# Holding back a batch's loads, with v in runs of four tokens, k chunks of every second row, and v's tail compact

## The chip, the cores and the metric

The kernel runs on one core of one Trainium2 chip. The metric is the device time of one execution in microseconds (us). A run is called slow when its time is over 1.5% above the fastest run of the same kernel in its job, and fast otherwise; the mean clock that the chip granted to the tensor engine is given beside it. Where not said otherwise, only fast runs are compared. Engine names follow the profile: PE is the tensor engine, PEld its weight loads, DVE the vector engine, ACT the scalar engine, POOL the general engine, SP the engine that here does nothing but start DMAs. "SPq" lines are DMAs that SP issued; their time is what the issue took on SP's own queue, not the time to landing.

## The reference

An attention layer with a learned feature map, then a gated linear unit with a causal convolution of five taps. Shapes: 8 batches, 8 heads, 576 tokens, head size 64, 128 features, model size 512, all float32.

```python
def _attn_ref(q, k, v, w_phi):
    def phi(x):
        proj = np.einsum('bhsd,df->bhsf', x, w_phi)
        proj = proj - np.max(np.abs(proj), axis=-1, keepdims=True)
        return np.concatenate([np.exp(proj), np.exp(-proj)], axis=-1)
    q_p, k_p = (phi(q), phi(k))
    kv = np.einsum('bhsf,bhsd->bhfd', k_p, v)
    z = np.sum(k_p, axis=2)
    num = np.einsum('bhsf,bhfd->bhsd', q_p, kv)
    den = np.einsum('bhsf,bhf->bhs', q_p, z)[..., None] + 1e-06
    return (num / den).astype(np.float32)

def _moe_ref(x, w_val, conv_w, w_out):
    # gate = sigmoid(causal convolution of x with conv_w, 5 taps, per channel)
    # val = x @ w_val
    return (gate * val @ w_out).astype(np.float32)
```

## The kernel before

The main loop is a pipeline of three stages over batches. Iteration i makes the features of k and q of batch i, the attention of batch i-1 and the gated unit (called MLP below) of batch i-2. The instructions of the stages are interleaved in the program, so PE's queue holds them in one fixed order.

First, k and q are cast to bfloat16 by POOL into a scratch buffer in DRAM, and SP reads them back with a transposing DMA. A batch's loads and transposes are put into the program at the start of the iteration before.

```python
def load_rows(st, src, name, parts):
    b = st.b
    T = qtp.tile([P, H * HALF], BF16, name=name)
    rows = src[b].rearrange("h s d -> h (s d)").rearrange("h (i x) -> i h x", x=256)
    hn = H // parts
    for c in range(parts):
        R = dram.tile([hn * 2 * P, 2 * D], BF16, name=f"{name}R{parts}")
        nc.gpsimd.dma_start(
            R[:, :].rearrange("(h i y) x -> i h (y x)", h=hn, y=2), rows[0:P, c * hn:(c + 1) * hn, :],
        )
        nc.sync.dma_start_transpose(T[:, c * hn * 2 * P:(c + 1) * hn * 2 * P], R[:, :])
    # ... the same for the tail (the last 64 tokens of each head), name "...Rt"
```

Second, v comes by plain DMAs on SP: two for the main part, and eight small ones for the tail, into a tile with zeros between the heads, so that one matmul can serve four heads.

```python
    for hq in range(4):
        for g in range(2):
            nc.sync.dma_start(
                st.VNt[32 * hq:32 * hq + 32, 2 * g:2 * g + 2, hq, :],
                v[b, 4 * g + hq, 4 * P:S, :].rearrange("(r t) d -> r t d", t=2),
            )
```

Third, the features come in five units, u = 4 (the tail) first. POOL multiplies v by the exponentials of each unit (tile VT; VTt for the tail), and PE accumulates k features times v in `unit_kv`.

Fourth, the results leave by `unit_out`, three times per batch. ACT copies a PSUM tile into an SBUF tile OUTs, and SP stores it. The pool that OUTs comes from has two buffers. All PSUM tiles share one pool of four.

```python
    mlp = ctx.enter_context(tc.tile_pool(name="mlp", bufs=2))
    ps2 = ctx.enter_context(tc.tile_pool(name="ps2", bufs=4, space=bass.MemoryType.PSUM))
    # ...
def unit_out(st, w):
    # ... matmuls into OUTp ...
    OUTs = mlp.tile([P, 2, DM], FP32, name="OUTs")
    nc.scalar.activation(OUTs[0:m, 0:len(cs), :], OUTp[0:m, 0:len(cs), :], AF.Copy)
    for n, c in enumerate(cs):
        # ... (two, three and one store for w = 0, 1 and 2)
            nc.sync.dma_start(ob[par, i0:i0 + k, :], OUTs[n0 - P * c:n0 - P * c + k, n, :])

for i in range(B + 2):
    # sa, sb, sc: states of batches i, i-1, i-2
    if i + 1 < B:
        load_qk(states[i + 1])
        load_v(states[i + 1])
    if sa:
        alloc_A(sa)
        alloc_B(sa)
    merge(units_features(sa) if sa else [], units_mlp(sc) if sc else [])
    if i == 0:
        late_constants()
    num = units_num(sb) if sb else []
    if sa:
        unit_mrows(sa)
        kv = units_kv(sa)
        merge(units_q(sa), num[0:3] + kv[0:1] + num[3:6] + kv[1:2] + num[6:])
```

Of the kernel before, what the change touches and what calls it, by code (L numbers as in the profile page):

```python
# [19 lines left out]
P = 128  # L20
# [13 lines left out]
def kernel(  # L34
# [13 lines left out]

    nc = tc.nc
# [19 lines left out]
    def load_rows(st, src, name, parts):  # L69
        b = st.b  # L70
        T = qtp.tile([P, H * HALF], BF16, name=name)
        rows = src[b].rearrange("h s d -> h (s d)").rearrange("h (i x) -> i h x", x=256)
        hn = H // parts
        for c in range(parts):
            R = dram.tile([hn * 2 * P, 2 * D], BF16, name=f"{name}R{parts}")
            nc.gpsimd.dma_start(
                R[:, :].rearrange("(h i y) x -> i h (y x)", h=hn, y=2), rows[0:P, c * hn:(c + 1) * hn, :],
            )
            nc.sync.dma_start_transpose(T[:, c * hn * 2 * P:(c + 1) * hn * 2 * P], R[:, :])  # L79
        R = dram.tile([H * NT, 2 * D], BF16, name=f"{name}Rt")  # L80
        nc.gpsimd.dma_start(
            R[:, :].rearrange("(h i y) x -> i h (y x)", h=H, y=2), rows[P:HALF // 2, :, :],
        )
        nc.sync.dma_start_transpose(T[:, TAIL:H * HALF], R[:, :])
        return T

    VNT = []
    for s in range(2):
        t = const.tile([P, 4, 4, D], FP32, name=f"VNT{s}")
        VNT.append(t)  # L90

    def load_v(st):
        b = st.b
        st.VN = vnp.tile([P, 2, H, 2, D], FP32, name="VN")
        st.VNt = VNT[b % 2]
        for j in range(2):
            nc.sync.dma_start(
                st.VN[:, j, :, :, :],
                v[b, :, 2 * P * j:2 * P * (j + 1), :].rearrange("h (p t) d -> p h (t d)", t=2),
            )  # L100
        for hq in range(4):
            for g in range(2):
                nc.sync.dma_start(
                    st.VNt[32 * hq:32 * hq + 32, 2 * g:2 * g + 2, hq, :],
                    v[b, 4 * g + hq, 4 * P:S, :].rearrange("(r t) d -> r t d", t=2),
                )

    def load_qk(st, parts=1):
        st.KT = load_rows(st, k, "KT", parts)
        st.QT = load_rows(st, q, "QT", parts)  # L110

    load_qk(states[0], 2)


# [38 lines left out]
    for s in range(2):  # L153
# [3 lines left out]
    HMASK = const.tile([P, 4], FP32, name="HMASK")  # L157
    nc.vector.tensor_reduce(
        HMASK[:, :], ident_f[:, :].rearrange("p (x r) -> p x r", x=4), AX.X, ALU.add,
    )  # L160
    for s in range(2):
        nc.gpsimd.memset(VNT[s][:, :, :, :], 0.0)

    load_v(states[0])

# [22 lines left out]
    def group_matmuls(T, PS, u):  # L188
        nx = 4 if u < 4 else 2
        for x in range(nx):  # L190
            if u < 4:
                c0 = (4 * (u % 2) + x) * 2 * P + P * (u // 2)
            else:
                c0 = TAIL + P * x
            for par in range(2):
                nc.tensor.matmul(  # L196
                    PS[:, par, x, :], T[ROWS[par], c0:c0 + P], W2[ROWS[par], :],
                    start=True, stop=True,
# [3 lines left out]
    def alloc_A(st):  # L202
        st.MQb = MQBS[st.b % 2]
# [5 lines left out]
        st.VTt = vtp.tile([P, 2, 4, 4, E1], BF16, name="VTt")  # L209

    def unit_k(st, u):
        PK = ps2.tile([P, 2, 4, F], FP32, name="PK", tag="b")
        nx = group_matmuls(st.KT, PK, u)
# [13 lines left out]
        with nc.allow_low_precision("bf16 scaled v"):  # L227
            if u < 4:
                VNu = st.VN[:, u // 2, 4 * (u % 2):4 * (u % 2) + 4, :, :].rearrange("p x t d -> p (x t) d")
                nc.gpsimd.tensor_tensor(  # L230
                    st.VT[:, :, sl, 0:D], VNu.unsqueeze(1).to_broadcast([P, 2, 8, D]),
                    EK[:, :, :].unsqueeze(3).to_broadcast([P, 2, 8, D]), ALU.mult,
                )
                nc.gpsimd.tensor_copy(st.VT[:, :, sl, D:E1], EK[:, :, :].unsqueeze(3))  # L234
                return
            for sgn in range(2):
                EKb = EK[:, sgn, :].unsqueeze(2).unsqueeze(3)
                nc.gpsimd.tensor_tensor(
                    st.VTt[:, sgn, :, :, 0:D], st.VNt[:, :, :, :],
                    EKb.to_broadcast([P, 4, 4, D]), ALU.mult,  # L240
                )
                nc.gpsimd.tensor_tensor(
                    st.VTt[:, sgn, :, :, D:E1],
                    HMASK[:, :].unsqueeze(1).unsqueeze(3).to_broadcast([P, 4, 4, 1]),
                    EKb.to_broadcast([P, 4, 4, 1]), ALU.mult,
                )

    def unit_qmax(st, u):
        PQ = ps2.tile([P, 2, 4, F], FP32, name="PQA", tag="b")
        n = group_matmuls(st.QT, PQ, u)  # L250
# [54 lines left out]
    def alloc_B(st):  # L305
        st.XN, st.GS = {}, {}
        st.KVSB = kvp.tile([P, 2, 2, 4, E1], BF16, name="KVSB")
# [4 lines left out]
    def unit_kv(st, g):  # L312
        KVPS = ps2.tile([P, 2, 512], FP32, name="KVPS", tag="b")
        for sgn in range(2):
            for x in range(4):
                for jp in range(4):
                    s = (jp // 2) * 16 + 8 * g + 2 * x + jp % 2
                    nc.tensor.matmul(  # L318
                        KVPS[:, sgn, x * E1:(x + 1) * E1],
                        st.KTIL[:, sgn, s, :], st.VT[:, sgn, s, :],  # L320
                        start=(x == 0 and jp == 0), stop=False, skip_group_check=True,
                    )
            for par in range(2):
                nc.tensor.matmul(  # L324
                    KVPS[:, sgn, 0:4 * E1], st.KTIL[:, sgn, 32 + 2 * g + par, :],
                    st.VTt[:, sgn, 2 * g + par, :, :],
# [196 lines left out]
```

## Time and profile before

| | before |
|---|---|
| three runs at first | 347.88, 359.19, 361.25 us |
| profiled run | 358.38 us (span 356.6), mean clock 0.875, a slow run |
| first GATE matmul of batches 0, 1, 2, 3 | 93.5, 145.6, 179.5, 213.5 us |
| PE busy | 251.8 us, 71% of the span |

The profile fell in a slow run.

The first GATE matmul of a batch marks where its MLP begins; the distance from one to the next is the time per batch.

The page of before shows the busy share of PE and the granted clock in 40 equal slices of the span, in tenths:

```profile
PE   0004374149896009898999889898989897989793
...
PEclk9999998556999557997899699969996999699897
```

PE is idle in slices 14 and 15 (some 116 to 134 us). The timeline of SP explains it (start, duration, engine and line, operation, output<-input, how many):

```profile
98.64 13.25 SPq L79 DMA_TRANSPOSE KT<-KTR_1436  x1
...
113.29 8.68 SPq L79 DMA_TRANSPOSE QT<-QTR_1443  x1
...
123.78 5.07 SPq L103 DMA_DIRECT2D VNT_90<-in_v_dram  x8
128.94 4.87 SPq L427 DMA_DIRECT2D out_dram<-OUTs  x6
```

The six output stores come last, behind 30 us of load issues. ACT's timeline shows what they hold up: two OUTs copies at 108.6, and the third only when a store has landed (in brackets: idle time before, and what ended it).

```profile
108.60 1.94 ACT L421 ACTIVATE OUTs<-OUTp 128x1024 f32<-128x1024 f32 x2
...
132.65 0.59 ACT L421 ACTIVATE OUTs<-OUTp 64x512 f32<-64x512 f32 x1 [20.00 <-DMA out_dram<-OUTs]
```

PE follows, because its next PSUM tile is the one that this copy would release:

```profile
113.35 0.81 PE L344 MATMUL NUM<-KVSB,QTIL 128*128 128x65 bf16 x21
133.29 0.59 PE L367 MATMUL XTP<-ident_bf,XN 128*128 128x128 bf16 x4 [19.13 <-ACT OUTs L421]
```

The table of waits has the same events as totals (us in all, times, longest), beside PE's wait at the start:

```profile
PE PK L196 <- DMA KT<-KTRt: 26.0, 1, 26.0
...
ACT OUTs L421 <- DMA out_dram<-OUTs: 24.9, 4, 20.0
...
PE XTP L367 <- ACT OUTs L421: 19.9, 2, 19.1
```

It is one event of 19 us and a few of about one. Why were the queues so full there? POOL's timeline: between 83 and 111 us it issued the casts of four batches; the first and the last of k:

```profile
83.24 0.93 POOL L76 DMA_DIRECT2D KTR_1436<-in_k_dram  x1
...
104.47 0.93 POOL L76 DMA_DIRECT2D KTR_3062<-in_k_dram  x1
```

From 145.6 us on the run is regular. A table of stretches (from:to, length, then busy time and number of instructions of PE, PEld, DVE, ACT and POOL, then granted clock, DMA share, GB/s):

```profile
179.50:213.50 34.00, 31.01 (x359) 19.25 (x360) 21.76 (x31) 22.66 (x32) 13.54 (x18) 0.90 0.47 108
```

PE is busy 31.0 us of each 34.0 us. It is the limit here, at a clock of 0.90. SP's timeline in the same stretch:

```profile
195.69 4.01 SPq L427 DMA_DIRECT2D out_dram<-OUTs  x6
...
201.83 5.98 SPq L79 DMA_TRANSPOSE KT<-KTR_3062  x1
```

### The profile page before, as it was taken

To read this page: it belongs to the slowest core of one execution; us is meant where nothing else is said; L and a number is where in the kernel's file an instruction comes from. 1 tells how busy PE (TensorE), PEld (TensorE's weight loads), DVE (VectorE), ACT (ScalarE), POOL (GpSimd) and SP (SyncE) were. 2 spreads that over 40 slices of the span, in tenths; PEclk is the share of its full clock that TensorE was granted. 3 is DMA by queue.
4 is the path that set the end of the run, shared out by engine and by line. 5 is a ranking of instruction groups with operands and counts; after the bars stand their busy time and mean duration, and the time that the engine had idled before them with its cause. 6 is when DMAs were issued, how large, how long until landed. Compare 5 with 4: busy or idle time off the path is not lost.

```text
span 356.6 us, 6909 instructions
## 1 busy us (share of the span) xinstructions
PE 251.8 (71%) x2868; PEld 158.2 (44%) x2876; DVE 176.4 (49%) x253; ACT 189.3 (53%) x277; POOL 142.0 (40%) x191
## 2 busy tenths in 40 slices
PE   0004374149896009898999889898989897989793
PEld 0003142125663006554664556356635663665571
DVE  2007507244586004685567566845874586341630
ACT  1005777447566017477757755857586567733122
POOL 8201693999397000454056306520761257000000
PEclk9999998556999557997899699969996999699897
DMA  9994929999999979305630781160030003001203
GB/s 185 171 211 110 172 27 213 151 176 184 182 198 188 173 181 199 70 15 170 150 68 15 228 136 30 68 194 3 0 119 18 2 0 119 17 0 45 91 0 132
DMA packets 85321, 39.32 MB, mean 110 GB/s; under 512 B 44709, under 2 KB 80677, under 8 KB 85290
## 3 DMA queue, kind: packets, MB, share of 16 engines
q1 hardware_dynamic: 65088, 28.32, 35.7%
q0 software_dynamic: 20032, 10.49, 22.1%
q8 instruction: 22, 0.36, 0.5%
q10 hardware_dynamic: 170, 0.08, 0.1%
q14 instruction: 9, 0.07, 0.1%
HBM read 30.48 MB, written 18.87 MB: 138 GB/s over the span
## 4 chain that ended last, share of the span: by engine, by line
PE 55%; DVE 11%; SPq 9%; DMA 8%; POOL 7%; issue 4%; ACT 4%; ACTq 0%; POOLq 0%
PE GATE L386 12%; PE VAL L398 8%; PE OUTp L415 7%; PE KVPS L318 6%; PE NUM L344 5%; SPq L79 5%; PE XTP L367 4%; DVE MK L215 4%; PE PQ L277 3%; POOL VT L230 3%; DVE XN L353 3%; DMA out_dram<-OUTs 3%; PE PQ L272 3%; ACT KTIL L220 2%; PE KVPS L324 2%
## 5 line engine op out<-in xcount | busy, mean ns | idle before, releaser
L220 ACT ACTIVATE KTIL<-PK 128x1024 bf16<-128x1024 f32 (+1 forms) x80 | 70.7, 937 | 49.6 <-DVE MK L215 49.2
L282 ACT ACTIVATE QTIL<-PQ 128x1024 bf16<-128x1024 f32 x64 | 60.8, 1023 | 21.8 <-PE PQ L277 21.8
L215 DVE TENSOR_REDUCE MK<-PK 128x8 f32<-128x1024 f32 (+1 forms) x40 | 44.5, 1112 | 27.6 <-PE PK L196 27.6
L224 POOL TENSOR_SCALAR MK<-MK 128x8 f32<-128x8 f32 (+1 forms) x40 | 9.5, 239 | 118.4 <-DVE MK L215 118.3
L386 PE MATMUL GATE<-XT,DIAG 128*128 128x288 bf16 x320 | 46.0, 291 | 2.5 <-DVE XT L374 2.5
L391 ACT ACTIVATE GS<-GATE 128x576 bf16<-128x576 f32 x32 | 20.9, 652 | 39.1 <-PE GATE L386 39.1
L403 DVE SCALAR_TENSOR_TENSOR GV<-GS,VAL 128x576 bf16<-128x576 bf16 x32 | 24.1, 755 | 32.3 <-PE VAL L398 27.3
L367 PE MATMUL XTP<-ident_bf,XN 128*128 128x128 bf16 (+1 forms) x160 | 17.9, 245 | 29.3 <-ACT OUTs L421 19.9
L196 PE MATMUL PK<-W_127,KT 64*128 64x128 bf16 x288 | 16.9, 234 | 30.6 <-DMA KT<-KTRt 26.0
L415 PE MATMUL OUTp<-WOUT,GV 128*128 128x512 bf16 (+1 forms) x152 | 38.0, 382 | 0.4
L398 PE MATMUL VAL<-XT,WVAL 128*128 128x288 bf16 x256 | 37.5, 289 | 0.0
L421 ACT ACTIVATE OUTs<-OUTp 128x1024 f32<-128x1024 f32 (+1 forms) x24 | 20.4, 882 | 30.4 <-DMA out_dram<-OUTs 24.9
L386 PEld LDWEIGHTS <-DIAG 128*128 128x128 bf16 x320 | 29.6, 99 | 13.0 <-DVE XT L374 2.7
L318 PE MATMUL KVPS<-VT,KTIL 128*128 128x65 bf16 x512 | 29.4, 220 | 5.6 <-POOL VT L234 5.3
L318 PEld LDWEIGHTS <-KTIL 128*128 128x128 bf16 x512 | 26.2, 115 | 13.3 <-issue 9.4
L367 PEld LDWEIGHTS <-XN 128*128 128x128 bf16 (+1 forms) x160 | 10.4, 109 | 41.5 <-issue 20.5
L353 DVE TENSOR_TENSOR XN<-NUM,RCP 128x512 bf16<-128x512 f32 (+1 forms) x40 | 27.6, 690 | 1.4
L398 PEld LDWEIGHTS <-WVAL 128*128 128x128 bf16 x256 | 24.3, 99 | 7.8
L330 DVE CAST KVSB<-KVPS 128x520 bf16<-128x520 f32 x16 | 11.2, 700 | 33.4 <-PE KVPS L324 33.4
L196 PEld LDWEIGHTS <-KT 64*128 64x128 bf16 x288 | 10.3, 102 | 38.1 <-DMA KT<-KTRt 26.0
L252 DVE TENSOR_REDUCE MQB_144<-PQA 128x8 bf16<-128x1024 f32 (+1 forms) x20 | 22.3, 1114 | 9.0 <-PE PQA L196 8.8
L372 DVE COPY XT<-XTP 128x1024 bf16<-128x1024 bf16 x16 | 11.0, 690 | 31.5 <-PE XTP L367 31.5
(196 smaller groups left out, 374.8 us busy)
## 6 DMA issues: line engine op xcount, KB each, us to landing
VN<-in_v_dram SPq DMA_DIRECT2D x16, 512.0 KB, 5.6
out_dram<-OUTs SPq DMA_DIRECT2D x24, 256.0 KB, 2.3
out_dram<-OUTs SPq DMA_DIRECT2D x8, 192.0 KB, 2.3
out_dram<-OUTs SPq DMA_DIRECT2D x8, 128.0 KB, 2.3
KTRt<-in_k_dram POOLq DMA_DIRECT2D x8, 64.0 KB, 11.4
QTRt<-in_q_dram POOLq DMA_DIRECT2D x8, 64.0 KB, 12.0
KTR_165<-in_k_dram POOLq DMA_DIRECT2D x1, 512.0 KB, 11.8
QTR_172<-in_q_dram POOLq DMA_DIRECT2D x1, 512.0 KB, 15.3
```

The source lines that it names most:

```text
L196: nc.tensor.matmul(PS[:, par, x, :], T[ROWS[par], c0:c0 + P], W2[ROWS[par], :], start=True, stop=True,)
L215: nc.vector.tensor_reduce(st.MK[:, 1, sl].rearrange("p (x t) -> p t x", t=2), PK[:, :, 0:nx, :], AX.X, ALU.max, apply_absolute_value=True,)
L220: nc.scalar.activation(st.KTIL[:, sgn, sl, :].rearrange("p (x t) f -> p t x f", t=2), PK[:, :, 0:nx, :], AF.Exp, scale=1.0 - 2.0 * sgn,)
L252: nc.vector.tensor_reduce(st.MQb[:, :].rearrange("p (t s) -> p t s", t=2)[:, :, 4 * u:4 * u + n], PQ[:, :, 0:n, :], AX.X, ALU.max, apply_a ...
L282: nc.scalar.activation(st.QTIL[:, sgn, u, :, :, :], PQ[:, :, :, :], AF.Exp, scale=1.0 - 2.0 * sgn,)
L318: nc.tensor.matmul(KVPS[:, sgn, x * E1:(x + 1) * E1], st.KTIL[:, sgn, s, :], st.VT[:, sgn, s, :], start=(x == 0 and jp == 0), stop=False, ...
L353: nc.vector.tensor_tensor(XN[0:m, :, :].rearrange("p (g x) d -> p g x d", g=2), NUMv[:, :, :, 0:D], RCP[0:m, :, :].unsqueeze(3).to_broadca ...
L367: nc.tensor.transpose(XTP[:, dt, n, 0:m], XNf[0:m, dt * P:(dt + 1) * P], ident_bf[0:m, 0:m],)
L386: nc.tensor.matmul(GATE[:, par, 0:HALF], DIAG[:, jt, tap, :], XT[:, jt, t % 2, i0:i0 + HALF], start=(tap == 0), stop=(tap == 4),)
L398: nc.tensor.matmul(VAL[:, par, 0:HALF], WVAL[:, dt, jt * P:(jt + 1) * P], XT[:, dt, par, PAD:PAD + HALF], start=(dt == 0), stop=(dt == 3),)
L403: nc.vector.scalar_tensor_tensor(out=st.GV[jt][:, :, :], in0=GS[:, :, :], scalar=1.0, in1=VAL[:, :, 0:HALF], op0=ALU.add, op1=ALU.mult,)
L415: nc.tensor.matmul(OUTp[0:m, n, :], st.GV[jt][:, :, :].rearrange("p t i -> p (t i)")[:, P * c:P * c + m], WOUT[:, jt, :], start=(jt == 0), ...
```

## The change

The intent: load v in longer runs (four tokens, 1 KB, instead of two) with fewer DMAs for its tail; take every second column of the k tile so that k's rows match v's order; drop the zeros of v's tail and use matmuls of 32 rows instead; make the tail the last unit rather than the first; and hold a batch's loads back until the first VT product of the batch before it, so that POOL no longer runs several batches ahead. The core of the diff:

```diff
     def load_v(st):
         b = st.b
-        st.VN = vnp.tile([P, 2, H, 2, D], FP32, name="VN")
-        st.VNt = VNT[b % 2]
-        # ... two DMAs for VN, eight for VNt
+        st.VN = vnp.tile([P, H, 4, D], FP32, name="VN")
+        st.VNt = vnp.tile([P, 2, 2, D], FP32, name="VNt")
+        with tc.issue_after(st.k_last):
+            for hh in range(2):
+                nc.sync.dma_start(
+                    st.VN[:, 4 * hh:4 * hh + 4, :, :],
+                    v[b, 4 * hh:4 * hh + 4, 0:4 * P, :].rearrange("h (p c) d -> p h (c d)", c=4),
+                )
+            # ... two DMAs for VNt
@@ group_matmuls
-                c0 = (4 * (u % 2) + x) * 2 * P + P * (u // 2)
+                c0 = (4 * (u % 2) + x) * 2 * P
+                c0 += u // 2 if step == 2 else P * (u // 2)
+                cols = slice(c0, c0 + step * (P - 1) + 1, step)      # step 2 for k, 1 for q
@@ unit_k
+                    st.vt_ops[u] = nc.gpsimd.tensor_tensor(...).ins  # VT, one product per sign
@@ unit_kv, the tail
-                nc.tensor.matmul(
-                    KVPS[:, sgn, 0:4 * E1], st.KTIL[:, sgn, 32 + 2 * g + par, :],
-                    st.VTt[:, sgn, 2 * g + par, :, :], ...
+                        r = slice(32 * (2 * xp + xi), 32 * (2 * xp + xi) + NT)
+                        nc.tensor.matmul(
+                            KVPS[:, xi, c0:c0 + E1], st.KTIL[r, sgn, 32 + 2 * g + par, :],
+                            st.VTt[r, sgn, 2 * g + par, :], ...
@@ units_features
-        for u in (4, 0, 2, 1, 3):
+        for u in (0, 2, 1, 3, 4):
@@ the main loop
-        if i + 1 < B:
-            load_qk(states[i + 1])
-            load_v(states[i + 1])
         if sa:
             alloc_A(sa)
             alloc_B(sa)
         merge(units_features(sa) if sa else [], units_mlp(sc) if sc else [])
         if i == 0:
             late_constants()
+        if i + 1 < B:
+            with tc.issue_after(sa.vt_ops[0]):
+                load_k(states[i + 1])
+                load_v(states[i + 1])
+                load_q(states[i + 1])
```

The state tile KVSB is laid out by pairs of heads, batch 0 loads k, v, q in this order, and the zeroing of the old tail tiles is gone.

More of the change, by code (lines that the diff above doesn't have):

```diff
@@ L71, in load_rows @@
         T = qtp.tile([P, H * HALF], BF16, name=name)
-        rows = src[b].rearrange("h s d -> h (s d)").rearrange("h (i x) -> i h x", x=256)
+        flat = src[b].rearrange("h s d -> h (s d)")
+        main = flat[:, 0:2 * P * 2 * D].rearrange("h (i x) -> i h x", x=2 * 2 * D)
+        tail = flat[:, 2 * P * 2 * D:S * D].rearrange("h (i x) -> i h x", x=2 * 2 * D)
         hn = H // parts
@@ L76, in load_rows @@
             nc.gpsimd.dma_start(
-                R[:, :].rearrange("(h i y) x -> i h (y x)", h=hn, y=2), rows[0:P, c * hn:(c + 1) * hn, :],
+                R[:, :].rearrange("(h i y) x -> i h (y x)", h=hn, y=2), main[:, c * hn:(c + 1) * hn, :],
             )
@@ L80, in load_rows, with load_k, load_q @@
         R = dram.tile([H * NT, 2 * D], BF16, name=f"{name}Rt")
-        nc.gpsimd.dma_start(
-            R[:, :].rearrange("(h i y) x -> i h (y x)", h=H, y=2), rows[P:HALF // 2, :, :],
-        )
-        nc.sync.dma_start_transpose(T[:, TAIL:H * HALF], R[:, :])
-        return T
-    VNT = []
-    for s in range(2):
-        t = const.tile([P, 4, 4, D], FP32, name=f"VNT{s}")
-        VNT.append(t)
+        nc.gpsimd.dma_start(R[:, :].rearrange("(h i y) x -> i h (y x)", h=H, y=2), tail)
+        last = nc.sync.dma_start_transpose(T[:, TAIL:H * HALF], R[:, :])
+        return T, last.ins
+    def load_k(st, parts=1):
+        st.KT, st.k_last = load_rows(st, k, "KT", parts)
+    def load_q(st, parts=1):
+        st.QT, _ = load_rows(st, q, "QT", parts)
     def load_v(st):
         b = st.b
-        st.VN = vnp.tile([P, 2, H, 2, D], FP32, name="VN")
-        st.VNt = VNT[b % 2]
-        for j in range(2):
-            nc.sync.dma_start(
-                st.VN[:, j, :, :, :],
-                v[b, :, 2 * P * j:2 * P * (j + 1), :].rearrange("h (p t) d -> p h (t d)", t=2),
-            )
-        for hq in range(4):
+        st.VN = vnp.tile([P, H, 4, D], FP32, name="VN")
[6 more added lines that the diff above has]
+                )
             for g in range(2):
                 nc.sync.dma_start(
-                    st.VNt[32 * hq:32 * hq + 32, 2 * g:2 * g + 2, hq, :],
-                    v[b, 4 * g + hq, 4 * P:S, :].rearrange("(r t) d -> r t d", t=2),
-                )
-    def load_qk(st, parts=1):
-        st.KT = load_rows(st, k, "KT", parts)
-        st.QT = load_rows(st, q, "QT", parts)
-    load_qk(states[0], 2)
+                    st.VNt[:, g, :, :],
+                    v[b, 4 * g:4 * g + 4, 4 * P:S, :].rearrange("h (r t) d -> h r (t d)", t=2),
+                )
+    load_k(states[0], 2)
+    load_v(states[0])
+    load_q(states[0], 2)
     ident_bf = const.tile([P, P], BF16, name="ident_bf")
@@ L156 @@
         MQBS.append(t)
-    HMASK = const.tile([P, 4], FP32, name="HMASK")
-    nc.vector.tensor_reduce(
-        HMASK[:, :], ident_f[:, :].rearrange("p (x r) -> p x r", x=4), AX.X, ALU.add,
-    )
-    for s in range(2):
-        nc.gpsimd.memset(VNT[s][:, :, :, :], 0.0)
-    load_v(states[0])
     WVAL = const.tile([P, 4, DM], BF16, name="WVAL")
@@ L186, with group_matmuls @@
     ROWS = (slice(0, D), slice(D, 2 * D))
-    def group_matmuls(T, PS, u):
+    def group_matmuls(T, PS, u, step):
         nx = 4 if u < 4 else 2
@@ L191, in group_matmuls @@
             if u < 4:
-                c0 = (4 * (u % 2) + x) * 2 * P + P * (u // 2)
+                c0 = (4 * (u % 2) + x) * 2 * P
+                c0 += u // 2 if step == 2 else P * (u // 2)
+                cols = slice(c0, c0 + step * (P - 1) + 1, step)
             else:
-                c0 = TAIL + P * x
+                cols = slice(TAIL + P * x, TAIL + P * x + P)
             for par in range(2):
                 nc.tensor.matmul(
-                    PS[:, par, x, :], T[ROWS[par], c0:c0 + P], W2[ROWS[par], :],
-                    start=True, stop=True,
+                    PS[:, par, x, :], T[ROWS[par], cols], W2[ROWS[par], :], start=True, stop=True,
                 )
@@ L202, in alloc_A @@
     def alloc_A(st):
+        st.vt_ops = {}
         st.MQb = MQBS[st.b % 2]
@@ L208, in alloc_A @@
         st.VT = vtp.tile([P, 2, 32, E1], BF16, name="VT")
-        st.VTt = vtp.tile([P, 2, 4, 4, E1], BF16, name="VTt")
+        st.VTt = vtp.tile([P, 2, 4, E1], BF16, name="VTt")
     def unit_k(st, u):
         PK = ps2.tile([P, 2, 4, F], FP32, name="PK", tag="b")
-        nx = group_matmuls(st.KT, PK, u)
+        nx = group_matmuls(st.KT, PK, u, 2)
         sl = slice(8 * u, 8 * u + 2 * nx)
@@ L228, in unit_k @@
             if u < 4:
-                VNu = st.VN[:, u // 2, 4 * (u % 2):4 * (u % 2) + 4, :, :].rearrange("p x t d -> p (x t) d")
+                jj, hh = u // 2, u % 2
+                for sgn in range(2):
+                    st.vt_ops[u] = nc.gpsimd.tensor_tensor(
+                        st.VT[:, sgn, sl, 0:D].rearrange("p (x t) d -> p x t d", t=2),
+                        st.VN[:, 4 * hh:4 * hh + 4, 2 * jj:2 * jj + 2, :],
+                        EK[:, sgn, :].rearrange("p (x t) -> p x t", t=2)
+                        .unsqueeze(3).to_broadcast([P, 4, 2, D]), ALU.mult,
+                    ).ins
+                VT = st.VT[:, :, sl, :]
+            else:
                 nc.gpsimd.tensor_tensor(
-                    st.VT[:, :, sl, 0:D], VNu.unsqueeze(1).to_broadcast([P, 2, 8, D]),
-                    EK[:, :, :].unsqueeze(3).to_broadcast([P, 2, 8, D]), ALU.mult,
-                )
-                nc.gpsimd.tensor_copy(st.VT[:, :, sl, D:E1], EK[:, :, :].unsqueeze(3))
-                return
-            for sgn in range(2):
-                EKb = EK[:, sgn, :].unsqueeze(2).unsqueeze(3)
-                nc.gpsimd.tensor_tensor(
-                    st.VTt[:, sgn, :, :, 0:D], st.VNt[:, :, :, :],
-                    EKb.to_broadcast([P, 4, 4, D]), ALU.mult,
-                )
-                nc.gpsimd.tensor_tensor(
-                    st.VTt[:, sgn, :, :, D:E1],
-                    HMASK[:, :].unsqueeze(1).unsqueeze(3).to_broadcast([P, 4, 4, 1]),
-                    EKb.to_broadcast([P, 4, 4, 1]), ALU.mult,
-                )
+                    st.VTt[:, :, :, 0:D],
+                    st.VNt[:, :, :, :].rearrange("p g t d -> p (g t) d").unsqueeze(1).to_broadcast([P, 2, 4, D]),
+                    EK[:, :, :].unsqueeze(3).to_broadcast([P, 2, 4, D]), ALU.mult,
+                )
+                VT = st.VTt
+            nc.gpsimd.tensor_copy(VT[:, :, :, D:E1], EK[:, :, :].unsqueeze(3))
     def unit_qmax(st, u):
         PQ = ps2.tile([P, 2, 4, F], FP32, name="PQA", tag="b")
-        n = group_matmuls(st.QT, PQ, u)
+        n = group_matmuls(st.QT, PQ, u, 1)
         with nc.allow_low_precision("bf16 max"):
@@ L306, in alloc_B @@
         st.XN, st.GS = {}, {}
-        st.KVSB = kvp.tile([P, 2, 2, 4, E1], BF16, name="KVSB")
+        st.KVSB = kvp.tile([P, 4, 2, 2, E1], BF16, name="KVSB")
         st.XT = xtp.tile([P, 4, 2, PAD + HALF], BF16, name="XT")
@@ L310, in alloc_B, with unit_kv @@
         st.GV = [mlp.tile([P, 2, HALF], BF16, name="GV", tag=f"GV{jt}", bufs=2) for jt in range(4)]
-    def unit_kv(st, g):
+    def unit_kv(st, xp):
         KVPS = ps2.tile([P, 2, 512], FP32, name="KVPS", tag="b")
-        for sgn in range(2):
-            for x in range(4):
-                for jp in range(4):
-                    s = (jp // 2) * 16 + 8 * g + 2 * x + jp % 2
-                    nc.tensor.matmul(
-                        KVPS[:, sgn, x * E1:(x + 1) * E1],
-                        st.KTIL[:, sgn, s, :], st.VT[:, sgn, s, :],
-                        start=(x == 0 and jp == 0), stop=False, skip_group_check=True,
-                    )
-            for par in range(2):
-                nc.tensor.matmul(
-                    KVPS[:, sgn, 0:4 * E1], st.KTIL[:, sgn, 32 + 2 * g + par, :],
-                    st.VTt[:, sgn, 2 * g + par, :, :],
-                    start=False, stop=(par == 1), skip_group_check=True,
-                )
+        for xi in range(2):
+            x = 2 * xp + xi
+            for g in range(2):
+                for sgn in range(2):
+                    c0 = (2 * g + sgn) * E1
+                    for jp in range(4):
+                        s = 8 * (2 * (jp // 2) + g) + 2 * x + jp % 2
+                        nc.tensor.matmul(
+                            KVPS[:, xi, c0:c0 + E1], st.KTIL[:, sgn, s, :], st.VT[:, sgn, s, :],
+                            start=(g == 0 and sgn == 0 and jp == 0), stop=False, skip_group_check=True,
+                        )
+        for g in range(2):
+            for sgn in range(2):
+                c0 = (2 * g + sgn) * E1
+                for par in range(2):
+                    for xi in range(2):
+                        r = slice(32 * (2 * xp + xi), 32 * (2 * xp + xi) + NT)
+                        nc.tensor.matmul(
+                            KVPS[:, xi, c0:c0 + E1], st.KTIL[r, sgn, 32 + 2 * g + par, :],
+                            st.VTt[r, sgn, 2 * g + par, :],
+                            start=False, stop=(g == 1 and sgn == 1 and par == 1), skip_group_check=True,
+                        )
@@ L329, in unit_kv @@
         with nc.allow_low_precision("bf16 kv"):
             nc.vector.tensor_copy(
-                st.KVSB[:, g, :, :, :].rearrange("p s x e -> p s (x e)"), KVPS[:, :, 0:4 * E1],
+                st.KVSB[:, 2 * xp:2 * xp + 2, :, :, :].rearrange("p x g s e -> p x (g s e)"),
+                KVPS[:, :, 0:4 * E1],
             )
@@ L344, in unit_num @@
                     nc.tensor.matmul(
-                        NUM[0:m, g, x * E1:(x + 1) * E1], lhsT, st.KVSB[:, g, sgn, x, :],
+                        NUM[0:m, g, x * E1:(x + 1) * E1], lhsT, st.KVSB[:, x, g, sgn, :],
                         start=(sgn == 0), stop=(sgn == 1),
@@ L456, in units_kv @@
     def units_kv(st):
-        return [(2.0, lambda g=g: unit_kv(st, g)) for g in range(2)]
+        return [(2.0, lambda xp=xp: unit_kv(st, xp)) for xp in range(2)]
     def merge(ua, ub):
```

## The prediction

> **What bounds the kernel now.** From 145.6 us on it is regular: the chain of waits shows batches 34.0 us apart (first GATE at 179.5, 213.5, 247.4, 281.5); the stretch table gives PE 31.0 us busy of each 34, clock 0.90, against ACT 22.7, DVE 21.7, POOL 13.5. There PE is the limit. The loss is before that:
>
> 1. Start: PE's first matmul is at 26.0 us (waits: KT<-KTRt, 26.0). The first unit is the k tail, whose transpose is issued third, at 13.5 us, though the first main chunk's was issued at 8.1.
> 2. POOL chain of batch 0: two VTt products of 1.89 us, four VT of 1.9, from 40.1 to 52.1 us.
> 3. 60 to 83 us: POOL waits 5.8 us for WOUT, scales it 5.4 us, then issues loads of later batches between products; PE idles 8.2 us once.
> 4. 114 to 133 us: PE idles 19.1 us. POOL in order of time ran ahead: from 83 to 111 us it issued loads of batches 4 to 7. One k transpose holds the SP queue 13.3 us, a q transpose 8.7, eight VNT loads 5.1, and output stores stand behind them until 128.9 us; OUTs, then PSUM, then PE wait. [...]
>
> **What the change does.**
> - Loads of the next k and q come behind the first VT product of the current batch: POOL runs one batch ahead only. A batch's loads (3.5 MB at the 180 GB/s seen) take about 20 us by estimate, against 34 per batch. Item 4 should go: -15 to -20 us. Cost: a late q would stall PE.
> - Tail unit last, v of batch 0 behind k: first matmul at about 17 us. q still lands at about 27, and DVE (1.2 us per reduce) bounds the stage: -4 to -8 us.
> - v tail: eight issues of about 0.65 us on SP become two, 5.1 -> 1.3 us per batch; v main in runs of 1 KB, not 512 B.
> - POOL: the tail's 4.3 us become about 1.2 (by proportion to 1.9 us per 1024 elements)[...]. Net -2.7 us per batch, critical only in batches 0 and 1: with item 3, -3 to -8 us. The WOUT wait remains and may delay batch 1's loads.
> - PE: 8 tail matmuls of N=260 per batch become 32 of 32 rows, N=65 (NUM's run at 34 ns)[...]: -0.2 to +0.8 us per batch. [...]
> - ACT, DVE: as before.
>
> **Sum.** First GATE at about 80 us (93.5 now), six batches of 34.2 us without the stall, 41 us for the end as now: about 328; with some late q, 331. Before's 347.9 to 361.3 should be item 4 varying; after should vary less.
>
> Predicted 331 us, 318 to 346. Faster by over 2%: 0.88; within: 0.07; slower: 0.05.
>
> **Right if**: no wait of PE on OUTs above 5 us; POOL's loads one batch per 34 us; first matmul at 15 to 19 us; POOL busy about 120 us; batch distance 33.5 to 35.5 us from the third on. **Wrong if**: PE waits on KT or QT in each batch (distance above 36); strided weight loads clearly above 100 ns; the WOUT wait stands before batch 1's loads; stores still queue behind transposes on SP.

Three were allowances without a measurement behind them: for the split of VT on POOL, for the tiling of PE's array and for the stride of k's weights. The sum came to about 328 us, 331 with some late q. The terms are still inside the totals: the first in the -2.7 us on POOL (4.3 to 1.2 us alone makes -3.1), the second in the -0.2 to +0.8 us on PE. Measured for the first of them: after has two VT products of 1.05 us in place of one of 1.9. For the other two see "Why the prediction was wrong".

## The result, and the profile after

| | before | after |
|---|---|---|
| all runs, us | 347.88, 348.77 (fast), 359.19, 361.25 (slow) | 362.80, 362.96, 364.18, 365.15 (all fast) |
| median | 353.98 | 363.57 |
| ratio of fast runs | | 1.044 (1.037 to 1.051): slower |

A ratio is the mean time of one kernel's fast runs over that of the other's fast runs of the same rounds, so it is not quite the ratio of the medians. Predicted were 331 us and faster; measured is 4.4% slower, outside the range of 318 to 346. After's profile is of a fast run (365.15 us, span 363.4, mean clock 0.911).

First GATE matmul of each batch, in us, and the distances of the batches:

| | batch 0 | 1 | 2 | 3 | 4 | 5 | 6 | 7 |
|---|---|---|---|---|---|---|---|---|
| before (slow run) | 93.5 | 145.6 | 179.5 | 213.5 | 247.4 | 281.5 | 315.7 | 335.8 |
| after | 86.4 | 127.5 | 170.0 | 210.2 | 251.1 | 292.9 | 324.1 | 344.2 |
| distance, after | | 41.1 | 42.6 | 40.2 | 40.9 | 41.8 | 31.2 | 20.1 |

The start gained 7.1 us and the long distance from batch 0 to 1 went from 52.1 to 41.1 us. But the next five distances, 34.0 us each in before's slow run, add up to 196.6 us instead of 170.1. That is the loss: -7.1 - 11.0 + 26.5 - 1.6 (the end) = 6.8 us, the difference of the two spans. Against before's fast runs, of which there is no profile, the loss is larger; how their 10 us less are spread isn't known.

Note the sixth distance, 31.2 us. It falls in iteration 7, in which there is no next batch to load. The five long ones fall in iterations 2 to 6, which each load a batch.

The page of after, busy PE and granted clock by slices: PE's single hole has become one hole in each batch, and the clock drops after each.

```profile
PE   0013383598973899368981989368981989889793
...
PEclk9999999999995889859995899859996699999998
```

SP's timeline, one iteration:

```profile
157.24 0.54 SPq L428 DMA_DIRECT2D out_dram<-OUTs  x1
181.69 3.81 SPq L82 DMA_TRANSPOSE KT<-KTR_2322  x1
185.59 1.19 SPq L85 DMA_TRANSPOSE KT<-KTRt  x1
186.87 1.08 SPq L100 DMA_DIRECT2D VN<-in_v_dram  x2
188.05 1.22 SPq L105 DMA_DIRECT2D VNt<-in_v_dram  x2
189.37 4.16 SPq L82 DMA_TRANSPOSE QT<-QTR_2335  x1
193.63 1.19 SPq L85 DMA_TRANSPOSE QT<-QTRt  x1
194.91 4.20 SPq L428 DMA_DIRECT2D out_dram<-OUTs  x6
```

SP stands idle for 24 us, then everything comes at once, with the stores of this iteration at the end. The waits of SP's own queue say for what it stood (first line), and POOL's timeline says when that load was issued: at 175.5, after the VT product, as the change wants it.

```profile
SPq L82 <- DMA KTR_2322<-in_k_dram: 23.9, 1, 23.9
```

```profile
175.48 0.97 POOL L79 DMA_DIRECT2D KTR_2322<-in_k_dram  x1
```

ACT's timeline answers to before's. The first OUTs copies of the batch run at 185.8 us; the third finds both buffers unsaved and waits 7.15 us.

```profile
185.76 1.94 ACT L422 ACTIVATE OUTs<-OUTp 128x1024 f32<-128x1024 f32 x2
...
197.96 0.59 ACT L422 ACTIVATE OUTs<-OUTp 64x512 f32<-64x512 f32 x1 [7.15 <-DMA out_dram<-OUTs]
```

PE's timeline, the same moment:

```profile
191.03 0.40 PE L368 MATMUL XTP<-ident_bf,XN 128*128 128x128 bf16 x4 [0.52 <-DVE XN L354]
198.60 0.61 PE L264 MATMUL PQ<-QT,W_131 64*128 64x512 bf16 x2 [7.17 <-ACT OUTs L422]
```

The chain of work that ended last goes through just these pieces (start, duration, what):

```profile
189.74 0.78 PE NUM L345 x21
190.53 3.00 SPq L82
...
193.63 1.19 SPq L85
...
194.91 0.53 SPq L428
...
195.50 2.35 DMA out_dram<-OUTs
...
197.96 0.60 ACT OUTs L422
...
198.60 0.61 PE PQ L264 x2
```

Read it aloud: PE has nothing to do; the q transpose is still being issued on SP; then its tail; then the first store is issued and lands 2.35 us later; then ACT may copy; then PE may go on. As totals in the table of waits, with PE's wait for q at the start, which is new (its first wait, for k, went from 26.0 to 13.4 us):

```profile
ACT OUTs L422 <- DMA out_dram<-OUTs: 40.5, 7, 7.9
...
PE PQ L264 <- ACT OUTs L422: 37.4, 5, 7.9
...
PE PQA L189 <- DMA QT<-QTR_107: 12.1, 1, 12.1
```

One wait of 19 us has become five of about 7.5. The stretch table gives a whole batch, the hole, and what comes behind it:

```profile
173.20:213.40 40.20, 30.00 (x384) 18.93 (x384) 21.82 (x31) 22.71 (x34) 14.03 (x24) 0.87 0.61 119
191.40:198.60 7.20, 0.03 (x2) 0.05 (x1) 0.42 (x1) 0.64 (x2) 0.00 (x0) 0.58 1.06 241
198.60:203.00 4.40, 4.40 (x58) 2.78 (x59) 0.69 (x1) 2.79 (x3) 0.00 (x0) 0.52 0.24 67
```

For 7.2 us PE does nothing (0.03 us busy) while the DMA engines are full (a share of 1.06); then it works for 4.4 us at about half clock (0.52).

### The profile page after: what moved, and what is told of

It is laid out like the page before. It is cut to its first block, busy times and chain, and to the rows that moved or that the text cites. A ratio compares the mean times of both kernels' runs of the same rounds, so it can differ in the third digit from the quotient of the medians.

```text
span 363.4 us, 7234 instructions
## 1 busy us (share of the span) xinstructions
PE 250.0 (69%) x3068; PEld 159.9 (44%) x3068; DVE 174.9 (48%) x252; ACT 189.3 (52%) x277; POOL 121.9 (34%) x205
## 4 chain that ended last, share of the span: by engine, by line
PE 58%; DVE 9%; DMA 9%; SPq 8%; POOL 6%; issue 4%; ACT 4%; ACTq 0%; POOLq 0%
PE GATE L387 10%; PE OUTp L416 10%; PE VAL L399 8%; PE KVPS L314 6%; PE NUM L345 6%; SPq L82 5%; DMA out_dram<-OUTs 4%; PE PQ L269 4%; PE PQ L264 4%; DVE XN L354 3%; PE XTP L368 3%; DMA QT<-QTR_107 3%; POOL VT L224 3%; ACT KTIL L213 3%; DVE MK L208 2%
## 5 line engine op out<-in xcount | busy, mean ns | idle before, releaser
L274 ACT ACTIVATE QTIL<-PQ 128x1024 bf16<-128x1024 f32 x64 | 61.6, 1021 | 24.7 <-PE PQ L269 24.6
L264 PE MATMUL PQ<-QT,W_131 64*128 64x512 bf16 x64 | 17.0, 500 | 40.0 <-ACT OUTs L422 37.4
L244 DVE TENSOR_REDUCE MQB_146<-PQA 128x8 bf16<-128x1024 f32 (+1 forms) x20 | 22.3, 1115 | 19.4 <-PE PQA L189 19.4
L189 PE MATMUL PK<-W_131,KT 64*128 64x128 bf16 x288 | 17.5, 240 | 19.0 <-DMA KT<-KTR_91 13.4
L314 PE MATMUL KVPS<-VT,KTIL 128*128 128x65 bf16 x512 | 26.3, 219 | 5.3 <-POOL VT L238 5.1
L189 PE MATMUL PQA<-W_131,QT 64*128 64x128 bf16 x288 | 17.0, 240 | 17.8 <-DMA QT<-QTR_107 12.1
L314 PEld LDWEIGHTS <-KTIL 128*128 128x128 bf16 x512 | 24.0, 115 | 10.4 <-issue 7.5
L244 DVE TENSOR_REDUCE MQB_148<-PQA 128x8 bf16<-128x1024 f32 (+1 forms) x20 | 22.3, 1115 | 12.9 <-PE PQA L189 12.9
```

The source lines that it names most:

```text
L189: nc.tensor.matmul(PS[:, par, x, :], T[ROWS[par], cols], W2[ROWS[par], :], start=True, stop=True,)
L244: nc.vector.tensor_reduce(st.MQb[:, :].rearrange("p (t s) -> p t s", t=2)[:, :, 4 * u:4 * u + n], PQ[:, :, 0:n, :], AX.X, ALU.max, apply_a ...
L264: nc.tensor.matmul(PQ[:, par, :, :], W2[ROWS[par], :], QTm[ROWS[par], 4 * hh:4 * hh + 4, P * j:P * j + P], start=True, stop=False,)
L274: nc.scalar.activation(st.QTIL[:, sgn, u, :, :, :], PQ[:, :, :, :], AF.Exp, scale=1.0 - 2.0 * sgn,)
L314: nc.tensor.matmul(KVPS[:, xi, c0:c0 + E1], st.KTIL[:, sgn, s, :], st.VT[:, sgn, s, :], start=(g == 0 and sgn == 0 and jp == 0), stop=Fals ...
```

## The experiments

Theory S (stores): the loss comes from the hold-back alone, through SP's queue. The held k load reaches SP late, all issues that stand behind it in SP's order are late, the stores are last of them, and two OUTs buffers are too few for three groups of stores per batch. The rivals: the new layout of v and k and the 32-row matmuls cost the time; or PE is really short of q and k, which come late. If S holds, more OUTs buffers repair the changed kernel, dropping the hold-back repairs it too, and the hold-back put into the old kernel reproduces the loss. The rivals expect none of the three.

All twelve kernels were correct against the reference, and all their profiles are of fast runs. Three jobs, four kernels each, on three chips. In each job before itself ran seven times, three to six of them slow.

### First job: where the loss comes from

Before in the same job: 346.5, 348.6, 349.3 us (fast), 352.9 to 360.8 (four slow).

**Four OUTs buffers in the changed kernel (a_outs4).** Everything else as after.

```diff
-        OUTs = mlp.tile([P, 2, DM], FP32, name="OUTs")
+        OUTs = mlp.tile([P, 2, DM], FP32, name="OUTs", bufs=4)
```

> The changed kernel with four OUTs buffers in place of two. Theory S (the loss is the third store group of a batch: its OUTs buffer waits for stores that stand on the SP queue behind the held-back k and q transposes, and PE waits 7.2 to 7.9 us on the PSUM buffer in five batches): that wait goes, batches come 33 to 35 us apart instead of 40 to 41, 325 to 334 us. Rival P (the loss is on PE itself: 32-row tiles, strided weights, more matmuls): no change, 358 to 365 us. Rival L (k and q land late because they are held back): PE then waits on KT or QT instead, over 350 us.

Measured: 314.27 us median (313.43 to 315.62), ratio to before 0.904 (0.895 to 0.912). SP's timeline of one iteration has the stores still at the end, as late behind the transposes as in after, and ACT's timeline has the third OUTs copy running at once:

```profile
170.54 1.19 SPq L85 DMA_TRANSPOSE QT<-QTRt  x1
171.82 4.02 SPq L428 DMA_DIRECT2D out_dram<-OUTs  x6
```

```profile
164.94 0.59 ACT L422 ACTIVATE OUTs<-OUTp 64x512 f32<-64x512 f32 x1
```

The stretch table of one batch:

```profile
149.54:180.75 31.21, 28.20 (x384) 17.87 (x384) 21.77 (x31) 22.53 (x34) 14.00 (x24) 1.00 0.82 153
```

PE does the same 384 matmuls in 28.20 us at full clock instead of 30.00, and waits 3.0 us instead of 10.2. So of after's 40.2 us per batch, 7.2 were the wait and 1.8 the lower clock behind it. The five distances of batches 0 to 5 sum to 156.0 us against after's 206.4. That is 50.4 us, all of the difference of 49.3 us between the medians within about a microsecond (after ran in another job; before's fast runs are 346.5 to 349.3 us in both). In these five batches of after PE waits 37.4 us for OUTs and is busy 154.5 us instead of 141.0, which together makes it up. Theory S holds; the gain is larger than I expected, because I had kept 34 us per batch.

**The hold-back alone, in the old kernel (b_hold).** The layout, the matmuls and the order of units are before's; only the loads move.

```diff
-        if i + 1 < B:
-            load_qk(states[i + 1])
-            load_v(states[i + 1])
         # ... features and MLP of this iteration
+        if i + 1 < B:
+            with tc.issue_after(sa.vt_ops[0]):
+                load_qk(states[i + 1])
+                load_v(states[i + 1])
```

> The kernel before with only the hold-back: loads traced after the features of the current batch and ordered behind its first VT product. Theory S: the stores fall behind the transposes here too, and SP has eight VNT issues more per batch, so batches are 40 to 45 us apart and the time is 362 to 390 us. Rival P: as before, 345 to 362 us, or better for lack of the early stall.

Measured: 364.59 us (361.70 to 366.26), ratio 1.045 (1.027 to 1.064), the changed kernel's own. The waits have the same form, five times:

```profile
ACT OUTs L422 <- DMA out_dram<-OUTs: 41.5, 8, 8.2
...
PE XTP L368 <- ACT OUTs L422: 32.6, 5, 7.3
```

The hold-back alone is enough for the whole loss. The layout isn't needed for it.

**The changed kernel without the hold-back (a_nohold).** The loads go back to the start of the iteration, without the edge to the VT product.

```diff
+        if i + 1 < B:
+            load_k(states[i + 1])
+            load_v(states[i + 1])
+            load_q(states[i + 1])
         if sa:
             alloc_A(sa)
         # ...
-        if i + 1 < B:
-            with tc.issue_after(sa.vt_ops[0]):
-                ...
```

> The changed kernel with the loads traced where they were before and without the order edge behind the first VT product; everything else as changed. Theory S: no 7 us wait per batch, batches 33 to 35 us apart; POOL runs ahead again, so one stall of the early batches as before may come back; 328 to 348 us. Rival P: still over 40 us apart, 358 to 365 us.

Measured: 337.88 us (336.99 to 338.86), ratio 0.971 (0.963 to 0.980). One long wait of ACT's OUTs copy is back, 17.2 us, as in before, and the steady distance is 31.2 to 31.4 us (once 32.3):

```profile
ACT OUTs L422 <- DMA out_dram<-OUTs: 21.7, 5, 17.2
```

So with two OUTs buffers the hold-back costs 25.7 us (363.57 against 337.88, in two jobs): it trades one stall of 15 us for five of 7.5 us plus the clock behind each.

**The stores on ACT's queue (a_actstore).** If SP's order is the fault, another engine's queue should free the stores.

```diff
-                nc.sync.dma_start(ob[par, i0:i0 + k, :], OUTs[n0 - P * c:n0 - P * c + k, n, :])
+                nc.scalar.dma_start(ob[par, i0:i0 + k, :], OUTs[n0 - P * c:n0 - P * c + k, n, :])
```

> The changed kernel with the output stores issued from ACT in place of SP. Theory S: the stores no longer stand behind transposes; ACT pays six issues of about 0.65 us per batch, which its 11 us of idle time per batch hold; batches 34 to 36 us apart, 325 to 337 us. Rival P: 358 to 365 us. Rival L: over 350 us with PE waiting on KT or QT.

Measured: 351.85 and 351.88 us in its fast runs (357.72 and 357.90 slow), ratio 1.011 (0.994 to 1.029). Better than after, but far from the expected gain: a miss. ACT's timeline shows where the time goes.

```profile
182.75 7.16 ACTq L428 DMA_DIRECT2D out_dram<-OUTs  x5
189.96 1.08 ACT L213 ACTIVATE KTIL<-PK 128x512 bf16<-128x512 f32 x2 [7.34 <-DMA out_dram<-OUTs]
```

ACT computes nothing for 7 us, and PE stands behind its KTIL (22.3 us in five waits in the table of waits). It looks as if ACT issued slowly, but the row merges five issues and the time between them. Of the 48 stores on ACT the median issue took 0.41 us (view of the tile OUTs); in after, six on SP took 0.40 to 0.54 us each. Between the issues ACT waited. In this program, by the operands in the trace, each of these stores first waits until the last DMA that used the same completion semaphore (the counter that tells of a landing) has landed, and the stores share these semaphores with SP's loads. The third, fourth and fifth store were issued at 186.34, 187.97 and 189.56 us, each within 0.1 us of the landing of a v load on the same semaphore (186.26, 187.95, 189.54; these are in the operands and events of the packed trace, which the views don't print). The first two had waited for k's transposes in the same way (182.68, 183.05). The operands in after's packed trace are alike: the six stores from 194.91 us on wait for semaphores 109 to 114, which the two transposes of k and the four loads of v ahead of them (181.69 to 188.72 us) raise. The chain of work has the last of these loads:

```profile
182.84 6.69 DMA VNt<-in_v_dram
```

In iteration 7, where nothing is loaded, the five stores took 2.31 us together (from 294.56 us). So a queue that is free of transposes doesn't free the stores here, because they wait for the loads by way of the semaphores, and a compute engine pays for the wait. Stores with semaphores of their own were not tried.

### Second job: the parts apart

a_outs4 leaves a question. Its distance is 31.2 us, before's was 34.0, though neither waits for stores there. The expectations of this job weigh two explanations, under the letters O and K. Before in the same job: 346.7, 347.0, 349.5, 351.6 us (fast), 352.4 to 358.0 (three slow).

**Three OUTs buffers in the old kernel (b_outs3).** For the third, the small tile of the convolution weights was put into the first OUTs buffer; four were not run.

```diff
-    cw5 = const.tile([5, DM], FP32, name="cw5")
-    nc.scalar.dma_start(cw5[:, :], moe_conv_w[:, :])
+    cw5 = mlp.tile([P, 2, DM], FP32, name="OUTs", bufs=3)
+    nc.scalar.dma_start(cw5[0:5, 0, :], moe_conv_w[:, :])
@@ unit_out
-        OUTs = mlp.tile([P, 2, DM], FP32, name="OUTs")
+        OUTs = mlp.tile([P, 2, DM], FP32, name="OUTs", bufs=3)
```

> The kernel before with a third OUTs buffer (room is made by loading the conv weights into the first of them). Theory S says that the early stall of the kernel before, PE idle 19 us at 114 us, is the same queue on SP: the third OUTs of a batch waits for stores behind transposes. With a third buffer it should shrink to under 6 us; from the third batch on 34 us apart as before; 333 to 344 us, and less spread between runs. If the stall is DMA bandwidth alone, it stays: 346 to 360 us.

Measured: 324.64 us (321.49 to 325.76), ratio 0.928 (0.916 to 0.940), below the expected 333 to 344, because that had kept 34 us per batch. SP still issues that k transpose for 13.27 us, and its stores still come last, at 129.4 us. But nobody waits: the distance from batch 0 to batch 1 is 33.9 us (92.3 to 126.2) instead of 52.1. One batch of the steady part:

```profile
157.69:189.17 31.48, 28.23 (x359) 17.60 (x360) 21.67 (x31) 22.52 (x32) 13.55 (x18) 1.00 0.70 147
```

The old layout, the old matmuls and the old order also give 31.5 us, at a clock of 1.00. PE's 28.23 us here and 28.20 in a_outs4 say that the 32-row tail costs PE nothing. Before's 34.0 us are the same work at a clock of 0.90: 28.23 / 31.01 is 0.91.

**The tail as last unit in the old kernel (b_taillast).**

```diff
-        for u in (4, 0, 2, 1, 3):
+        for u in (0, 2, 1, 3, 4):
```

> The kernel before with the k and q tail units last in a batch's features in place of first. It asks why batches come 31.2 us apart in the changed kernel once the stores don't wait, against 34.0 before. Theory O (the last q reduce before the row maxima is half as long, so PE's gap there shrinks[...]): distance 31 to 32 us from the fourth batch on, clock 1.00 there, PE busy 28 us per batch. Theory K (it is the state matmuls, 32-row tiles for N=260): stays 34 us at clock 0.90. In the early part the first matmul comes at 17 us or earlier in both cases.

Measured: 336.71 us (334.69 to 337.20), ratio 0.962 (0.950 to 0.975). The long stall is still there (ACT's OUTs copy waits 17.0 us once); the first GATE comes at 87.5 us, and the steady distance is 31.4 to 31.6 us at a clock of 1.00. This is within 1.2 us of a_nohold, 337.88 us, in another job. So of the changed kernel's parts without the hold-back, the order of units makes the gain, and the layout nothing that shows.

**The tail as first unit in the repaired kernel (a4_tailfirst).** a_outs4 with the order of before.

```diff
-        for u in (0, 2, 1, 3, 4):
+        for u in (4, 0, 2, 1, 3):
```

> The changed kernel with four OUTs buffers and the tail units first again. Theory O: distance back to 33 to 34 us, clock 0.90, 328 to 340 us. Theory K: distance stays 31 to 32 us, and only the start is later: 316 to 324 us.

Measured: 324.40 us (323.17 to 327.57), ratio 0.930 (0.918 to 0.942), 10 us slower than a_outs4. Distances are 32 to 35 us, between the two expectations, and the table of waits names a cause that a_outs4 has not:

```profile
PE PQA L189 <- DMA QT<-QTRt: 16.2, 6, 10.1
```

The q tail is the last that lands of a held batch; used first, it stalls PE by about 1.2 us in five batches, beside the start. Here a late q costs something, as I had feared of the change itself. With the tail last it doesn't. The waits are not all of it: in four of the five batches from 115.5 us on PE is also busy some 29.6 us instead of 28.2, at a clock of 0.95. The start isn't later with the tail first: the first GATE comes at 82.0 us, in a_outs4 at 83.9.

**The repaired kernel without the hold-back (a4_nohold).** a_outs4 with the loads as in a_nohold (the same edit).

> The changed kernel with four OUTs buffers and without the hold-back. It asks what the hold-back is worth once stores can wait. If it is worth what I predicted of it (no crowding of DMA and POOL by loads of later batches): an early stall of 5 to 15 us remains here, 318 to 330 us, slower than the 314 us with it. If only the buffers mattered: 312 to 316 us.

Measured: 321.63 us (320.01 to 322.66), ratio 0.921 (0.911 to 0.930). That makes a table of two by two, medians of the kernel with the new layout:

| | two OUTs buffers | four OUTs buffers |
|---|---|---|
| loads early | 337.88 (a_nohold) | 321.63 |
| loads held back | 363.57 (after) | 314.27 (a_outs4) |

The sign of the hold-back depends on the buffers: +25.7 us with two, -7.4 us with four (the columns mix jobs; each kernel's own spread is 2 to 3 us). The 7 us lie in the early part: the first GATE is at 88.8 us against 83.9, and the batch behind it takes 34.3 us against 31.2. In POOL's timeline the early loads wait in line for a free scratch buffer, and hold POOL's products behind them:

```profile
90.35 0.88 POOL L79 DMA_DIRECT2D QTR<-in_q_dram  x1 [5.07 <-DMA QTR<-in_q_dram]
```

That was the run-ahead which the change was meant to end, and there the change does what it was meant to do.

As for the two explanations of 31.2 us: neither the layout nor the order is needed. b_outs3 and b_taillast reach 31.4 to 31.6 us with each of the two left as it was. What they share is a clock of 1.00. The clause in theory O that leads from PE's gap to its clock was not shown: PE's gap at that reduce is 1.32 us in before and 0.79 us in b_taillast, but b_outs3 has the 1.32 us too, at a clock of 1.00. Why before's slow run had 0.90 in that part is open (below). It isn't a matter of before's slow runs alone: in b_hold's profile, of a fast run, iteration 7 has neither loads nor a wait for stores, and still takes 33.9 us at 0.90.

### Third job: what is left, and the best version

Before in the same job: one fast run of 344.7 us and six slow ones of 350.8 to 361.3. The four kernels spread by 3.5 us at most.

**Three OUTs buffers and the tail last, old layout (b3_taillast).** The edits of b_outs3 and b_taillast together.

> The kernel before with a third OUTs buffer and the tail units last: what is left of the difference to the changed kernel without hold-back and with four buffers (321.6 us) is then the v layout and the 32-row tail matmuls. If the layout is worth what I costed on PE and POOL off the critical path (about 0.4 us per batch in the state matmuls, measured), this is 321 to 327 us. If tail last adds to the third buffer (324.6 us) as its earlier first matmul suggests, 315 to 321 us.

Measured: 321.08 us (319.57 to 322.42). Equal to a4_nohold's 321.63 us, within their spread, though in another job. These two differ in v's layout, the k chunks, the 32-row tail, the order of the loads and one OUTs buffer. Together these are worth nothing that can be seen, with the loads early.

**The factor 0.5 moved off POOL (a4_scale).** In batch 0 POOL waits for the output weights and multiplies them by 0.5, 5.4 us, in the middle of its products. ACT's copy can do it in the same time: one of 64x512 took 0.59 us with the factor (300.26 us in a4_scale) and 0.59 us without it (164.94 us in a_outs4).

```diff
-        nc.gpsimd.tensor_scalar_mul(WOUT[:, :, :], WOUT[:, :, :], 0.5)
@@ unit_out (bufs=4 as in a_outs4)
-        nc.scalar.activation(OUTs[0:m, 0:len(cs), :], OUTp[0:m, 0:len(cs), :], AF.Copy)
+        nc.scalar.activation(OUTs[0:m, 0:len(cs), :], OUTp[0:m, 0:len(cs), :], AF.Copy, scale=0.5)
```

> The changed kernel with four OUTs buffers, and the factor 0.5 taken from the product over WOUT on POOL (5.4 us) into the scale of the OUTs copy on ACT. The chain shows that product at 35.1 us, ahead of the VT products of batch 0. If it is critical there: 307 to 312 us against 314.3. If DVE or the late q bounds the start anyway: 312 to 315 us.

Measured: 307.42 us (307.17 to 310.64), 6.9 us below a_outs4. The first GATE moves from 83.9 to 77.3 us, which is 6.7 of them.

**All k units of batch 0 before its q units (a4_scale_kfirst).** In after, PE waits 12 us for q behind its first k unit.

```diff
+        if st.b == 0:
+            us += [(1.0, lambda u=u: unit_k(st, u)) for u in (0, 2, 1, 3, 4)]
+            return us + [(1.0, lambda u=u: unit_qmax(st, u)) for u in (0, 2, 1, 3, 4)]
```

> As a4_scale, and in batch 0 all five k units before the q units, since PE waits 11.5 us for the first q behind one k unit. The k reduces, exponentials and VT products then run during that wait: PE's second k unit at 15 to 18 us instead of 26; 303 to 310 us. If q's landing at 26 us and its five reduces bound the start: as a4_scale within 2 us.

Measured: 306.78 us (306.30 to 309.39), the same as a4_scale within 1 us. PE is through with batch 0's features at 39 us instead of 46.8, but batch 1's loads don't come earlier by as much: PE now waits 5.7 us for its k (at 45.0 us) and 7.5 us for its q (at 53.1). The gain turned into a new wait.

**The same, with v of batch 0 behind q (a4_best2).**

```diff
     load_k(states[0], 2)
-    load_v(states[0])
     load_q(states[0], 2)
+    load_v(states[0])
```

> As a4_scale_kfirst, and v of batch 0 loaded behind q in place of between k and q. q should land 2 to 4 us earlier, v later; 301 to 309 us if q bounds the start, slower than a4_scale_kfirst if the VT products do.

Measured: 307.55 us (306.68 to 308.15). No gain; the two waits stay, 7.3 and 7.5 us.

The best version is a4_scale or a4_scale_kfirst, which can't be told apart: 307 us, some 15% below the changed kernel (measured in another job), and 11% below before's one fast run of that job (307.42 / 344.71 is 0.892).

## Why the prediction was wrong

**The step that failed**, as the prediction put it: "Item 4 should go: -15 to -20 us. Cost: a late q would stall PE." The run-ahead did end, and with it the 13.3 us transpose (others of 512 KB took 1.2 to 6.0 us on SP in before's regular part and 3.7 to 4.7 us in after's; the median of those of 64 KB is 1.2 us). The stall did not go. It was a matter of which issues stand ahead of the stores on SP, and of how many OUTs buffers there are to wait with. In before's regular part the stores went out ahead of the next transposes (195.69 against 201.83 us); they stood behind them only in the one stall. The hold-back left the two buffers as they were and moved all of a batch's load issues to just before the stores, in each of five batches: 13.1 us of issues (181.69 to 194.82) that can't begin until the held k load lands. Measured in place of -15 to -20 us: the distance from batch 0 to 1, which holds the stall, shrank by 11.0 us, and five waits of about 7.5 us with a lower clock behind them made about 50 us against a_outs4.

**The cost that was named didn't occur.** From batch 2 on PE waits neither for q nor for k in after. In SP's fixed order the transposes had all the time they needed; it was what stood behind them that hadn't. The right reason stood in the last clause of the list of what could go wrong: "stores still queue behind transposes on SP". It had been seen in before's SP timeline, yet it got no term in the sum. What should have been asked: when the loads move, what else stands in the same queue, and behind what? In the program's text the stores even come before the held loads; in the built program, whose order the trace shows, they come after. The order of issue on an engine's queue is to be read from the trace or the built program and not from the text.

**A second term was of the wrong size.** "Six batches of 34.2 us" took the distance from a slow run with a clock of 0.90. Without stalls it is 31.2 to 31.6 us in every kernel here whose clock stayed at 1.00 (b_outs3, b_taillast, a_nohold, a_outs4). It hid that a repaired kernel would be 17 us faster than predicted.

**What was right.** The first matmul came at 13.4 us (predicted about 17, before 26.0), and PE then waited 12.1 us for q, which was there at 26.1 (predicted about 27). So the first GATE came 7.1 us earlier. That is the low end of the 7 to 16 us which the two items for the early part make together (4 to 8 and 3 to 8), and below the 13.5 us that the sum had. The wait for WOUT and its scaling indeed stayed, between batch 0's products, and a4_scale shows 6.9 us for it. POOL's busy time is 121.9 us (predicted about 120, before 142.0). The v tail's issues on SP went from 5.1 to 1.2 us per batch. The k weights read with stride 2 cost nothing: a weight load's median is 94 ns, as before. The 32-row tail cost nothing that shows: in a_outs4 16 of its matmuls between 128-row ones took 0.35 us (169.97 to 170.32 us), and PE's sum per batch is 28.20 us against 28.23 in b_outs3.

**Still open.** Why before itself has fast and slow runs. The prediction put it down to the stall of item 4 varying, and the runs don't support that: before spreads by 11 to 17 us in a job, but a_nohold and b_taillast, which keep the one long stall, spread by 1.9 and 2.5 us, no more than the kernels with three or four OUTs buffers (1.5 to 4.4). By an estimate, five distances of 34.0 us (before's slow profile) instead of 31.4 (b_taillast) make 13 us, so the lower clock in the regular part would be enough; no fast run of before was profiled. What tips the clock is open too: behind after's hole of 7.2 us it was 0.52; in before's slow run it was 0.50 from 200 to 206 us, with no PE gap longer than 1.32 us shortly ahead of it, while b_outs3, with the same gap, and a_outs4 passed the same place at 1.00. And two things were not tried: three buffers, not four, in the changed kernel; and the stores issued ahead of the transposes on SP.

## What to carry to other kernels

When a load is delayed, look at everything that stands behind it in the same in-order queue, not only at who needs the load; output stores there turned a late load into a late buffer here, and a late buffer into an idle tensor engine (in after 13.1 us of issues ahead of the stores, and 37.4 us of PE's waiting in five batches). Compare the number of output buffers with the number of store groups per round: with three groups and two buffers the store's delay was on the critical path here, and more buffers took it off: one more with the loads early, two more with the loads early or late. Stores on another engine's queue can still wait for loads: in a_actstore, where they share completion semaphores with them, five stores held ACT for 7.16 us. A row of the timeline that merges several issues holds the waits between them too (those 7.16 us, at a median of 0.41 us per issue).
